# A gated linear attention followed by a switch mixture of experts: experts ranked by count, rows turned on VectorE, products and moves rearranged

## The chip, the cores and the metric

The kernel runs on one core of one Trainium2 chip. The metric is device time in microseconds, the median of several runs; a profiled execution gives the span and everything inside it. All data are float32 in device memory.

## The reference

```python
# attention, (4, 8, 768, 48) each: q, k, v, a_re, a_im
mag = sqrt(a_re**2 + a_im**2); scale = minimum(mag, 0.999) / (mag + 1e-6)
for t in range(S):
    new_re = ar * S_re - ai * S_im
    new_im = ar * S_im + ai * S_re
    S_re, S_im = new_re + k[t] (outer) v[t], new_im
    y[t] = q[t] @ S_re
# x = y as (3072 tokens, 384)
logits = x @ w_gate                     # 8 experts
expert_idx = argmax(logits); gate_w = softmax(logits) at expert_idx
for e in range(8):
    h = maximum(x[mask] @ w1[e], 0)     # 384 x 1024
    out[mask] = gate_w[mask] * (h @ w2[e])   # 1024 x 384
```

## The kernel before

**Stage 1, attention** (0 to 239.8 us of the span). The complex decay is turned into magnitudes and angles along time, so that q and k are multiplied by decay and rotation, and a chunked linear attention follows. `front(u)` prepares one of ten units of time (`UNITS`, 128 to 384 steps of a batch; n = 3 x T columns, 1152 for a full unit). It loads gates (AB) and q, k (Z), takes logarithms and exponentials on ScalarE, and on VectorE runs two scans (L284 of the decay, L295 of the angle), the range reduction (L300, L301), the clipping L282, and the products by `mul` and `tt` (all at L150): im x c (here product 1), k x a, q x c (product 6), then z times cosine into `hz` and z times sine in place. Products 1 and 6 go to GpSimd (POOL) from unit `EARLY` = 3 on. The heads lie packed on 128 partitions (`BLOCKS`: p0, p1, g0, g1, h0, d0), and DMAs issued by SP (L334) move them to `hz`, with a real and an imaginary part for each head on 96 partitions: nine for a unit. `chunk(b, c)` does the attention of 128 steps on TensorE (L361 to L403), and `route` (L423 to L464) the gate, the expert and the place of each token; GpSimd scatters the rows into `xs_hbm`, where each expert has `CAP` = 448 places (L464). Places that may stay free are filled beforehand by DMAs from `empty`. The order of all this on every engine is a list written out by hand (`ORDER`, base 36 numbers of the operations), so an engine takes its work as listed, and waits where an input is late. After the last chunk some small VectorE operations and two products (L513 to L535) decide whether the slow, exact path `again` has to follow.

**Stage 2, experts** (239.8 us to the end). `expert(e)` loads w1 (L572), w2 (L574), 384 rows (L575) and the last 64 (L578) by SP. TensorE transposes the rows (L586), VectorE and ScalarE copy them out (L588). For each of eight hidden blocks three products with 448 columns (L597) follow and a rectification (L600, L603); three output blocks of 128 tokens take eight products of 384 columns each (L611). The 64 tokens behind 384 of two experts share one output bank (L626), one expert on each half of its partitions. VectorE applies the gate (L566), and GpSimd scatters into the output (L555). Here `Plan.order()` lists the operations, greedily by earliest start and then by longest tail, from the durations given to `M.add`. Three buffers hold w1 and three w2; xr, xrt and ht have two each. Two PSUM banks take transposes, three hidden blocks and three outputs. A product of L597, L611 or L626 in float32 leaves two records in the trace.

## Time and profile before

| | |
|---|---|
| median of 3 runs | 570.27 us (564.31 to 571.41) |
| profiled execution | 565.04 us, span 563.2 us |
| mean granted clock of TensorE | 0.967 |
| busy over the span | PE 86%, DVE 43%, ACT 38%, POOL 17% |
| attention | 0 to 239.8 us |
| experts | 239.8 us to the end |
| moved by DMA | 82.03 MB, mean 146 GB/s |

PE is TensorE, PEld its loading of weights, DVE VectorE, ACT ScalarE, POOL GpSimd and SP the engine that issues most DMAs (SPq in a timeline is its queue of commands). [...] The 16 DMA engines have a share of 1.00 when all are busy. The shares over the span are averages of two stages with different limits, so rows are read by stage. The duration of a matmul's record is modelled and overlaps its neighbours; starts are better compared with starts.

### The profile page before, as it was taken

Reading aid. Unit: us, or ns where it says so; the run is one execution under the profiler, and the core shown is the slowest. Engines: PE = TensorE matmul, PEld = TensorE weight load, DVE = VectorE, ACT = ScalarE, POOL = GpSimd, SP = SyncE. Lnnn points to the kernel's source line nnn. Section 1 sums busy time; section 2 is a strip of 40 time slices with the busy share of each in tenths; the row PEclk is TensorE's granted clock in tenths of the full one; section 3 lists DMA queues with packets and bytes.
Section 4 is the critical chain, followed back from the end, with each engine's and each line's share of the span. In section 5 each row is a group of like instructions: output and inputs, shape, how many; then the busy total and the mean of one; then the engine's idle time right before and its main releaser. Section 6 shows DMA issues by size and latency. Waiting matters only on the chain. (4 is left out here: it accounts for less than half of the span.)

```text
span 563.2 us, 7082 instructions
## 1 busy us (share of the span) xinstructions
PE 485.5 (86%) x2785; PEld 329.1 (58%) x2785; DVE 240.8 (43%) x412; ACT 214.0 (38%) x313; POOL 94.3 (17%) x106
## 2 busy tenths in 40 slices
PE   0045998798898799729999999999999999999995
PEld 0034997787798699614555555555555555555552
DVE  3999989989798684401111021110111011211011
ACT  6999898979788565201100011000011000111000
POOL 3012214206240533200001020020100010200022
PEclk9999999989799799959999999999999999999998
DMA  8486959578399865199502272214443021400010
GB/s 320 131 252 163 256 149 336 116 214 216 118 208 217 245 113 180 44 318 387 205 14 82 111 263 64 98 42 169 160 143 120 14 69 57 145 2 14 1 38 34
DMA packets 25384, 82.03 MB, mean 146 GB/s; under 512 B 3600, under 2 KB 16816, under 8 KB 20896
## 3 DMA queue, kind: packets, MB, share of 16 engines
q1 hardware_dynamic: 22016, 72.04, 42.8%
q0 software_dynamic: 3328, 9.47, 4.6%
q8 instruction: 24, 0.39, 0.3%
q14 instruction: 16, 0.13, 0.1%
HBM read 54.32 MB, written 12.62 MB: 119 GB/s over the span
## 5 line engine op out<-in xcount | busy, mean ns | idle before, releaser
L597 PE MATMUL bank<-xrt,w1b 128*128 128x448 f32 x384 | 149.4, 544 | 2.1 <-ACT xrt L588 2.1
L611 PE MATMUL bank<-w2b,ht 128*128 128x384 f32 x384 | 128.4, 488 | 0.0
L597 PEld LDWEIGHTS bank<-xrt,w1b 128*128 128x128 f32 x384 | 73.0, 192 | 70.5 <-issue 64.8
L611 PEld LDWEIGHTS bank<-w2b,ht 128*128 128x128 f32 x384 | 72.1, 190 | 51.9 <-issue 6.9
L603 ACT ACTIVATE ht<-bank 128x448 f32<-128x448 f32 x32 | 17.4, 544 | 174.0 <-PE bank L597 174.0
L555 POOL DMA_INDIRECT out_dram<-yo,xr x24 | 23.5, 978 | 292.2 <-DVE yo L566 288.1
L368 PE MATMUL bank<-hz 96*128 96x128 f32 x384 | 61.6, 315 | 7.7 <-DMA hz<-Z 6.5
L600 DVE TENSOR_SCALAR ht<-bank 128x448 f32<-128x448 f32 x32 | 20.0, 625 | 111.4 <-PE bank L597 111.4
L368 PEld LDWEIGHTS bank<-hz 96*128 96x128 f32 x384 | 54.8, 221 | 12.0 <-issue 6.1
L361 PE MATMUL bank<-ident,hz 96*128 96x96 f32 x160 | 23.6, 279 | 38.0 <-DMA hz<-Z 35.4
L566 DVE TENSOR_SCALAR yo<-bank,xr 128x384 f32<-128x384 f32 x24 | 14.8, 618 | 79.4 <-PE bank L611 79.4
L588 ACT COPY xrt<-bank 128x384 f32<-128x384 f32 x16 | 7.6, 478 | 94.0 <-PE bank L586 93.9
L361 PEld LDWEIGHTS bank<-ident,hz 96*128 96x128 f32 x160 | 18.7, 161 | 40.6 <-issue 38.1
L236 ACT ACTIVATE AB<-AB 128x1152 f32<-128x1152 f32 (+2 forms) x40 | 38.3, 968 | 7.1 <-DMA AB<-in_gates_u_dram 5.2
L150 DVE TENSOR_TENSOR am<-bank,causal 128x512 f32<-128x512 f32 x48 | 32.3, 680 | 14.5 <-PE bank L368 14.5
L150 DVE TENSOR_TENSOR Z<-Z,AB 128x1152 f32<-128x1152 f32 (+4 forms) x20 | 34.1, 1704 | 1.2 <-DMA hz<-Z 0.3
L403 PE MATMUL bank<-turn,yt 128*128 128x104 f32 x192 | 28.0, 292 | 6.7 <-ACT yt L391 3.9
L464 POOL DMA_INDIRECT xs_hbm<-xg,slot x24 | 26.1, 1088 | 40.1 <-DVE cumb L461 14.8
L150 POOL TENSOR_TENSOR AB<-AB,C 128x1152 f32<-128x1152 f32 (+2 forms) x7 | 18.0, 2567 | 87.3 <-ACT C L236 77.2
L387 PE MATMUL bank<-am,v 128*48 128x128 f32 x384 | 30.5, 299 | 2.2 <-DVE am L150 2.2
L395 PE MATMUL bank<-v,kt 128*96 128x48 f32 x320 | 31.6, 253 | 0.0
L395 PEld LDWEIGHTS bank<-v,kt 128*96 128x96 f32 x320 | 30.1, 171 | 1.8 <-issue 1.5
(110 smaller groups left out, 499.3 us busy)
## 6 DMA issues: line engine op xcount, KB each, us to landing
w1b<-in_w_dram SPq DMA_DIRECT2D x8, 1536.0 KB, 14.0
w2b<-in_w_dram SPq DMA_DIRECT2D x8, 1536.0 KB, 7.0
AB<-in_gates_u_dram SPq DMA_DIRECT2D x6, 1152.0 KB, 7.1
Z<-in_qk_u_dram SPq DMA_DIRECT2D x6, 1152.0 KB, 8.2
hz<-Z SPq DMA_DIRECT2D x12, 432.0 KB, 8.7
xr<-xs_hbm SPq DMA_DIRECT2D x8, 579.0 KB, 7.8
v<-in_v_dram SPq DMA_DIRECT2D x8, 576.0 KB
hz<-hz SPq DMA_DIRECT2D x6, 432.0 KB, 5.5
```

Of the source, the lines that this page charges most:

```text
L150: (eng or nc.vector).tensor_tensor(out=o, in0=a, in1=b, op=op)
L236: lambda: nc.scalar.activation(o, i, func=f, scale=scale, bias=bias, **kw), r, w, tag)
L361: nc.tensor.transpose(KT[hf][:, (h % 4) * 96:(h % 4) * 96 + 96], hk[:, h], ident[0:96, 0:96])
L368: nc.tensor.matmul(SC[hf][:, (h % 4) * 128:(h % 4) * 128 + 128], lhsT=hk[:, h], rhs=hq[:, h], start=True, stop=True)
L387: nc.tensor.matmul(YT[ps, (h // 2) * 128:(h // 2) * 128 + 128], lhsT=V[:, cl, h * D:h * D + D], rhs=am[2 * par + hf][:, h % 4, :], start=( ...
L395: nc.tensor.matmul(ST[0:96, h * D:h * D + D], lhsT=kt[par][:, h * 96:h * 96 + 96], rhs=V[:, cl, h * D:h * D + D], start=(c == 0 and h == 0 ...
L403: nc.tensor.matmul(XT[:, p * 104:p * 104 + 104], lhsT=yt[par][:, p * 128:p * 128 + 128], rhs=turn[:, p, :], start=True, stop=True)
L464: i = nc.gpsimd.indirect_dma_start(out=xs_hbm[:, :], out_offset=bass.IndirectOffsetOnAxis(ap=R[slot][:, c:c + 1], axis=0), in_=xg[:, (g0 + ...
L555: i = nc.gpsimd.indirect_dma_start(out=out[:, :], out_offset=bass.IndirectOffsetOnAxis(ap=index, axis=0), in_=y, in_offset=None, bounds_ch ...
L597: nc.tensor.matmul(HB[hb][:, 0:CAP], lhsT=w1b[ws][:, c:c + 128], rhs=xrt[s][:, d, :], start=(d == 0), stop=(d == DT - 1))
L600: M.add("DVE", 0.6, lambda f_=f_, hb=hb: nc.vector.tensor_scalar_max(ht[s][:, f_, :], HB[hb][:, 0:CAP], 0.0), (("H", hb),), (("ht", s, f_),))
L611: nc.tensor.matmul(OB[ob][:, 0:DM], lhsT=ht[s][:, f_, j * 128:j * 128 + 128], rhs=w2b[ws][:, f_ * DM:f_ * DM + DM], start=(f_ == 0), stop= ...
```

## The change

**In attention.** Heads 6 and 7 are packed so that their last 16 channels alternate on partitions 96 to 127, and the moves of a unit become seven (three real, four imaginary). Product 1 is always on VectorE; product 6 is on GpSimd from unit 1 on. Each GpSimd product waits, by an added dependence, for the last VectorE operation with `port=True` that the list has ahead of it. The fills become two of 80 places for each expert, from place `MINC` = 288 on. The first expert's weights (`wA1`, `wA2`, expert 0) are loaded in unit 4. The list `ORDER` is a new one (its numbers are not shown).

**Ranking.** After the last route, VectorE ranks the experts by count, expert 0 kept first, and `perm` holds the expert of each rank. SP reads it into a register (`values_load`) and addresses rows and weights by it. Rank r has `ROOM[r]` places (448, 448, 416 four times, 384, 384), and `again` also follows if a count exceeds its room.

**Experts.** The rows are loaded by four DMAs an expert, each to 32 partitions, with 288 numbers of a row in one piece; VectorE turns 32x32 blocks (`nc.vector.transpose`, three an expert) into what the products read. Gates and places come by DMAs of their own (`hg`, `hs`). The tokens behind 384 go to `hl`, and share two output banks: 64 each of ranks 0 and 1, 32 each of ranks 2 to 5. Hidden and output blocks have four PSUM banks each; w1b has two buffers and w2b five.

```diff
+BLOCKS = [x for g in range(3) for x in ((slice(0, 48), g, g, 0), (slice(48, 96), g, 3 + g, 0))]
+BLOCKS += [(slice(96, 128), 0, 6, 0), (slice(96, 128), 1, 7, 0), (slice(96, 128, 2), 2, 6, 32), (slice(97, 128, 2), 2, 7, 32)]
-EARLY = 3
+EARLY = 1
+ON_POOL = "6"
-MINC = 256
+MINC = 288
+FIRST = 0
+ROOM = (448, 448, 416, 416, 416, 416, 384, 384)
+LEFT = ((0, 0, 64, 0, 0), (1, 0, 64, 0, 64), (2, 0, 32, 1, 0), (3, 0, 32, 1, 32), (4, 0, 32, 1, 64), (5, 0, 32, 1, 96))
+XW = 288
...
-            mul(pool, n, im, im, c, (Bk, Ck), (Bk,))
+            mul(pool1, n, im, im, c, (Bk, Ck), (Bk,))
...
-            mul(pool, n, qq, qq, c, (Q, Ck), (Q,))
+            mul(pool6, n, qq, qq, c, (Q, Ck), (Q,))
...
+                pieces = ([(0, 48, 0)] if part else []) + [(48, 96, 3)]
+                todo = [(hz[slot][r0:r0 + D, h0:h0 + 3, :, off:off + T], src[p0:p1], range(h0, h0 + 3), 0) for p0, p1, h0 in pieces]
+                todo.append((hz[slot][r0:r0 + 32, 6:8, :, off:off + T], src[96:128, 0:2], (6, 7), 0))
+                todo.append((hz[slot][r0 + 32:r0 + 48, 6:8, :, off:off + T], src[96:128, 2], (6, 7), 32))
...
+                if u == 4:
+                    for o, src, k in ((wA1, w1, "wA1"), (wA2, w2, "wA2")):
+                        P.add("SP", 0.65, lambda o=o, src=src: nc.sync.dma_start(o, src[FIRST * 128:FIRST * 128 + 128, :]), (), (k,),
...
-                o["fn"]()
+                ins = o["fn"]()
+                if o["port"] and o["eng"] == "DVE":
+                    behind = ins
+                elif o["port"] and behind is not None:
+                    tc.add_manual_dep(ins.ins, behind.ins.name, mybir.DependencyInfo(mybir.DependencyClass.Sync, mybir.DependencyReason.DATA),
...
+            for q in range(4):
+                M.add("SP", 0.65, lambda q=q: nc.sync.dma_start(
+                    xr[s][32 * q:32 * q + 32, 0:nb, :], row(r, 0, 32 * nb).rearrange("(b p) w -> p b w", p=32)[:, :, 32 * q:32 * q + XW]),
...
+            for d in range(DT):
+                M.add("DVE", 0.00105 * nt + 0.06, lambda d=d: nc.vector.transpose(
+                    xrt[s][:, d, 0:nt].rearrange("p (b i) -> p b i", i=32), xr[s][:, 0:nb, d * 128:d * 128 + 32]),
...
-                        nc.tensor.matmul(HB[hb][:, 0:CAP], lhsT=w1b[ws][:, c:c + 128], rhs=xrt[s][:, d, :], start=(d == 0), stop=(d == DT - 1))
+                        nc.tensor.matmul(HB[hb][:, 0:nt], lhsT=a[:, c:c + 128], rhs=xrt[s][:, d, 0:nt], start=(d == 0), stop=(d == DT - 1))
...
+                    for rr, n, p0 in who:
+                        nc.tensor.matmul(OB[ob][p0:p0 + n, 0:DM], lhsT=hl[sh][:, f_, p0:p0 + n], rhs=w2_of(rr)[0][:, f_ * DM:f_ * DM + DM],
+                                         start=(f_ == 0), stop=(f_ == FT - 1), skip_group_check=True)
```

TensorE where the first expert passes into the second (L586 transposes, L597 hidden products, L611 outputs), before:

```order
L597 MATMUL bank_63<-xrt_1983,w1b_1975 128x448 x3
L586 MATMUL bank_61<-ident,xr_1982 128x128 x3
L586 MATMUL bank_62<-ident,xr_1982 128x128 x3
L597 MATMUL bank_64<-xrt_1983,w1b_1975 128x448 x3
L586 MATMUL bank_61<-ident,xr_1982 128x128 x3
L586 MATMUL bank_62<-ident,xr_1982 128x64 x3
L611 MATMUL bank_66<-w2b_1978,ht_1985 128x384 x4
L597 MATMUL bank_65<-xrt_1984,w1b_1976 128x448 x3
```

The same place after the change (L663 hidden products, L679 outputs; wA the early weights of the first expert):

```order
L663 MATMUL bank_61<-xrt_1996,wA_127 128x448 x3
L663 MATMUL bank_63<-xrt_1996,wA_127 128x448 x3
L663 MATMUL bank_62<-xrt_1997,w1b_1988 128x448 x3
L663 MATMUL bank_64<-xrt_1997,w1b_1988 128x448 x3
L663 MATMUL bank_61<-xrt_1997,w1b_1988 128x448 x3
L663 MATMUL bank_63<-xrt_1997,w1b_1988 128x448 x3
L663 MATMUL bank_61<-xrt_1997,w1b_1988 128x448 x3
L663 MATMUL bank_62<-xrt_1997,w1b_1988 128x448 x3
L663 MATMUL bank_63<-xrt_1997,w1b_1988 128x448 x3
L663 MATMUL bank_64<-xrt_1997,w1b_1988 128x448 x3
L679 MATMUL bank_65<-wA_128,ht_1998 128x384 x4
L679 MATMUL bank_66<-wA_128,ht_1998 128x384 x4
```

The transposes are gone, the first expert's products read weights that came in attention, and all hidden blocks of the second expert now stand ahead of the first expert's outputs.

The second shared group on TensorE after the change (L692; hl holds the hidden values of the tokens behind 384), the first six of 32 commands:

```order
L692 MATMUL bank_68<-w2b_1991,hl_2001 32x384
L692 MATMUL bank_68<-w2b_1992,hl_2001 32x384
L692 MATMUL bank_68<-w2b_1993,hl_2001 32x384
L692 MATMUL bank_68<-w2b_1989,hl_2001 32x384
L692 MATMUL bank_68<-w2b_1991,hl_2001 32x384
L692 MATMUL bank_68<-w2b_1992,hl_2001 32x384
```

Four experts' products of 32 columns stand one after another, where pairs of 64 stood in L626.

SP's commands at the start of the expert stage, before (L572 w1, L574 w2, L575 and L578 rows):

```order
L572 DMA w1b_1975<-in_w_dram 128x3072
L575 DMA xr_1981<-xs_hbm 128x3x386
L578 DMA xr_1981<-xs_hbm 64x386
L574 DMA w2b_1978<-in_w_dram 128x3072
L575 DMA xr_1982<-xs_hbm 128x3x386
L578 DMA xr_1982<-xs_hbm 64x386
```

After (L632 rows, L627 the register with the rank's expert, L636 w1; ISA computes an address):

```order
L632 DMA xr_1994<-xs_hbm 32x14x288 x4
L627 TENSOR_LOAD perm
L636 ISA
L636 DMA w1b_1988<-in_w_dram 128x3072
L632 ISA
L632 DMA xr_1995<-xs_hbm 32x14x288
```

Nothing stands ahead of the first rows now; the second expert's commands stand behind the register, and its w1 ahead of its rows.

GpSimd's products in attention, the first five before (AB by C is product 1, Z by C product 6):

```order
L150 TENSOR_TENSOR AB_125<-AB_125,C_131 128x1152
L150 TENSOR_TENSOR AB_126<-AB_126,C_132 128x1152
L150 TENSOR_TENSOR Z_128<-Z_128,C_131 128x3x384
L150 TENSOR_TENSOR AB_127<-AB_127,C_133 128x1152
L150 TENSOR_TENSOR Z_129<-Z_129,C_132 128x3x384
```

and after:

```order
L156 TENSOR_TENSOR Z_144<-Z_144,C_147 128x3x256
L156 TENSOR_TENSOR Z_145<-Z_145,C_148 128x3x384
L156 TENSOR_TENSOR Z_143<-Z_143,C_146 128x3x384
L156 TENSOR_TENSOR Z_144<-Z_144,C_147 128x3x384
L156 TENSOR_TENSOR Z_145<-Z_145,C_148 128x3x384
```

VectorE after the change, in the same part of attention:

```order
L294 SCALAR_TENSOR_TENSOR AB_140<-C_146,AB_140 128x1152
L156 TENSOR_TENSOR Z_145<-Z_145,AB_142 128x3x384
L315 TENSOR_SCALAR AB_142<-AB_142 128x1152
L156 TENSOR_TENSOR am_154<-bank_62,causal 128x512
L297 TENSOR_SCALAR AB_140<-AB_140 128x1152
L316 SCALAR_TENSOR_TENSOR AB_142<-AB_142 128x1152
L299 SCALAR_TENSOR_TENSOR AB_140<-AB_140,lend,C_146 128x384
L156 TENSOR_TENSOR AB_141<-AB_141,C_147 128x1152
```

Product 1 (the last row, AB_141 by C) has come to VectorE, where Z_145 by AB_142 is k x a, and GpSimd's row has product 6 alone.

## Rows read from the trace of the kernel before

**Rows 1.** Stage windows: us, busy per engine (records), granted PE clock, DMA share, GB/s.
```profile
28.00:141.00 113.00, 91.90 (x855) 82.67 (x855) 107.20 (x125) 102.61 (x129) 29.00 (x14) 0.98 0.77 213
...
239.80:252.90 13.10, 2.89 (x12) 2.07 (x13) 1.21 (x4) 0.96 (x2) 0.00 (x0) 0.50 0.96 325
252.90:557.20 304.30, 302.65 (x980) 163.20 (x980) 44.26 (x81) 23.79 (x46) 25.45 (x26) 1.00 0.29 103
...
168.96:183.04 14.08, 12.58 (x153) 11.91 (x153) 12.08 (x21) 11.94 (x20) 1.11 (x1) 1.00 1.00 217
...
255.90:270.20 14.30, 14.30 (x39) 7.17 (x38) 2.04 (x4) 1.63 (x3) 0.00 (x0) 1.00 1.00 401
```

**Rows 2.** Groups by line, expert stage: busy us, mean ns, idle before and releaser.
```profile
L597 PE MATMUL bank<-xrt,w1b 128*128 128x448 f32 x384 | 149.4, 544 | 2.1 <-ACT xrt L588 2.1
...
L626 PE MATMUL bank<-w2b,ht 128*64 128x384 f32 x128 | 21.5, 489 | 0.0
...
L586 PE MATMUL bank<-ident,xr 128*128 128x128 f32 (+1 forms) x96 | 14.4, 282 | 9.8 <-DMA xr<-xs_hbm 9.8
```

**Rows 3.** TensorE's timeline: start us, duration us, line, records, [idle <-releaser].
```profile
252.90 17.51 PE L597 MATMUL bank<-xrt,w1b 128*128 128x448 f32 x42 [0.50 <-ACT xrt L588]
...
330.57 16.05 PE L597 MATMUL bank<-xrt,w1b 128*128 128x448 f32 x42 [0.57 <-ACT xrt L588]
...
365.05 6.93 PE L597 MATMUL bank<-xrt,w1b 128*128 128x448 f32 x18
371.82 5.32 PE L611 MATMUL bank<-w2b,ht 128*128 128x384 f32 x16
...
406.71 16.02 PE L597 MATMUL bank<-xrt,w1b 128*128 128x448 f32 x42 [0.50 <-ACT xrt L588]
```

**Rows 4.** All engines, timeline where attention ends and the expert stage begins.
```profile
241.67 0.38 SPq L575 DMA_DIRECT2D xr<-xs_hbm  x1
...
249.52 2.89 PE L586 MATMUL bank<-ident,xr 128*128 128x128 f32 x12 [9.77 <-DMA xr<-xs_hbm]
```

**Rows 5.** The same view at the end of the span.
```profile
558.05 0.98 POOL L555 DMA_INDIRECT out_dram<-yo,xr  x1 [1.60 <-DVEq L645]
559.33 0.98 POOL L555 DMA_INDIRECT out_dram<-yo,hg  x1 [0.30 <-issue]
```

**Rows 6.** The same view in attention: products on GpSimd beside VectorE.
```profile
61.60 2.67 POOL L150 TENSOR_TENSOR Z<-Z,C 128x1152 f32<-128x1152 f32 x1 [11.43 <-ACT C L236]
61.69 1.92 DVE L295 TENSOR_TENSOR_SCAN AB<-bank,tend,AB 128x384 f32<-128x384 f32 x2
...
91.88 3.33 POOL L150 TENSOR_TENSOR AB<-AB,C 128x1152 f32<-128x1152 f32 x1 [3.73 <-DVE AB L300]
...
92.70 3.72 DVE L301 SCALAR_TENSOR_TENSOR AB<-AB 128x1152 f32<-128x1152 f32 x1
...
117.99 1.36 DVE L301 SCALAR_TENSOR_TENSOR AB<-AB 128x1152 f32<-128x1152 f32 x1
119.27 0.75 DVE L282 TENSOR_SCALAR AB<-AB 128x1152 f32<-128x1152 f32 x1
```

**Rows 7.** VectorE's groups by line and shape, 28 to 213.7 us.
```profile
L150 DVE TENSOR_TENSOR Z<-Z,AB 128x2304 f32<-128x2304 f32 x6 | 17.6, 2933 | 0.5
...
L150 DVE TENSOR_TENSOR hz<-Z,AB 128x2304 f32<-128x2304 f32 x6 | 15.3, 2550 | 1.7 <-ACT AB L236 1.6
L301 DVE SCALAR_TENSOR_TENSOR AB<-AB 128x1152 f32<-128x1152 f32 x6 | 10.5, 1753 | 0.1
...
L282 DVE TENSOR_SCALAR AB<-AB 128x1152 f32<-128x1152 f32 x6 | 6.7, 1113 | 0.0
...
L150 DVE TENSOR_TENSOR Z<-Z,C 128x1152 f32<-128x1152 f32 x1 | 1.4, 1351 | 0.0
```

**Rows 8.** The moves' line L334: count, issue ns (min/median/max), and landing.
```profile
L334 SPq DMA_DIRECT2D hz<-Z x50: 507/592/2177, 25.7 to 220.0; - x50
...
DMA to landing us min/median/max: 2.3/5.0/10.0
```

More of the change, by code (lines that the diff above doesn't have):

```diff
@@ L189, in gateloop_then_moe @@
     ones_b = const([128, 128], "ones_b", 1.0, BF16)
+    num_i = const([128, E], "num_i", dt=I32)
+    nc.gpsimd.iota(num_i, pattern=[[1, E]], base=0, channel_multiplier=0)
+    num = const([128, E], "num")
+    nc.vector.tensor_copy(num, num_i)
+    room = const([128, E], "room")
+    for r in range(E):
+        nc.gpsimd.memset(room[:, r:r + 1], float(ROOM[r]))
+    wA1, wA2 = const([128, DT * F], "wA1"), const([128, FT * DM], "wA2")
     cum = const([128, E], "cum")
@@ L329, in front @@
                     rd = (Q, K) if part else ht_
[L330 removed]
+                    if part and hs[0] == 0:
                         rd = rd + tuple(("hm", slot, cl + x) for x in range(nch))
[L332 removed]
+                    if not part and hs[0] == 3:
                         w = w + tuple(("hm", slot, cl + x) for x in range(nch))
[L334 to L335 removed]
@@ L336, in front @@
-                    moved.setdefault(u, []).append(i)
+                    P.add("SP", 0.65, lambda o=o, i_=i_: nc.sync.dma_start(o, i_), rd, w, lat=1.8,
+                          kb=2 * (48 if d0 == 0 and hs[0] < 6 else 32 if d0 == 0 else 16) * len(hs) * T * 4 / 1e3, rate=(200.0, 250.0, 280.0)[nch - 1])
         def load_v(b, half):
@@ L499, in gateloop_then_moe @@
                             route(b, r0, r1)
+            behind = None
             for i in P.order(ORDER):
@@ new lines, in expert @@
+        def expert(r):
+            nt = ROOM[r]
+            nb = nt // 32
+            s = r % 2
+            (a, ka), (w, kw) = w1_of(r), w2_of(r)
+            for d in range(DT):
+                M.add("DVE", 0.00105 * nt + 0.06, lambda d=d: nc.vector.transpose(
+                    xrt[s][:, d, 0:nt].rearrange("p (b i) -> p b i", i=32), xr[s][:, 0:nb, d * 128:d * 128 + 32]),
+                    tuple(("xr", s, q) for q in range(4)), (("xrt", s, d),))
+            mine = [(k, n, sh, p0) for rr, k, n, sh, p0 in LEFT if rr == r]
@@ L637, in gateloop_then_moe @@
+        with tc.manual_schedule():
+            M.add("SP", 0.0, lambda: None, (), ("perm",))
+            loads(0)
+            for r in range(E):
+                if r + 1 < E:
+                    loads(r + 1)
+                expert(r)
+                for sh in range(2):
+                    if max(x[0] for x in LEFT if x[3] == sh) == r:
+                        shared(sh)
+                if r < E - 1:
                     M.add("POOL", 1.0, lambda: nc.gpsimd.drain(), ("scattered",), ("drained",))
-                if e == 2:
+                if r == 2:
@@ L756, in _layout @@
         z = _np.zeros((B, 128, G, S), a.dtype)
-        for p0, p1, g0, g1, h0, d0 in BLOCKS:
-            z[:, p0:p1, g0:g1] = a[:, h0:h0 + g1 - g0, :, d0:d0 + p1 - p0].transpose(0, 3, 1, 2)
+        for sl, g, h, d0 in BLOCKS:
+            n = len(range(128)[sl])
+            z[:, sl, g] = a[:, h, :, d0:d0 + n].transpose(0, 2, 1)
         a = z
```

295 lines of the change are left out of this document (154 added, 141 removed).

## The prediction

> **What bounds the kernel now.** I read the stage windows first, then the groups of the expert stage by line, then TensorE's own timeline there, and last the hand-over between the stages, the end, and the collisions of VectorE and GpSimd. The windows split the span in three. From 28 to 141 us VectorE is busy 107.2 of 113.0 us and ScalarE 102.6: attention is bound by those two. From 239.8 to 252.9 us TensorE works 2.9 of 13.1 us: it waits for the first expert's rows. From 252.9 to 557.2 us it is busy 302.65 of 304.3 us with DMA share 0.29: a pure TensorE bound [rows 1]. So a product taken out of that last stretch shortens the kernel by its whole length, and the same holds for VectorE's work up to 141 us. What goes beside these costs nothing.
>
> The reader should take cadences and not mean durations, since matmuls overlap: 18 records of L597 from 365.05 to 371.82 us are 6.77 us, 0.376 us for each record of 448 columns, against a mean of 544 ns by line [rows 2, 3].
>
> **Narrower rooms.** There are 384 records of L597 [rows 2]: 384 x 0.376 = 144.4 us. Columns fall from 3584 to 3328 (the sum of ROOM), so 144.4 x 256/3584 = **-10.3 us**. The products of L611 stay (3 x 128 tokens an expert). The rooms hold if the counts fit; the inputs give 354 tokens to the first expert and 421, 406, 403, 392, 388, 370, 338 to the rest in order, so the slow path is not entered.
>
> **Transposes off TensorE.** L586 is busy 14.4 us [rows 2], of which 2.89 us lie ahead of the first product [rows 4]; 11.5 us lie in the bound stretch. The first product behind a copied block also waits for ScalarE, 0.50 us at 406.71 us [rows 3], 2.1 us in all of which 0.5 at the start [rows 2]. So 13.1 us would go if no records overlapped; they do, at both ends of each of some fifteen groups. Between 11.5 and 13.1 I take **-11.8 us**, near the busy time. The work that replaces them, three transposes of up to 448 elements an expert on VectorE, is in no trace here: an estimate of 0.3 to 0.6 us each. From 252.9 us on VectorE is busy 44.3 of 304.3 us [rows 1] and the rows land an expert ahead, so they are hidden; without this cover one expert's three would cost at most 2 us, 14 us over seven.
>
> **Leftover tokens.** Four shared groups cost 21.5 us for 128 records, 5.4 us for the 32 of each [rows 2]. In such a group the two 64-wide products of a pair run side by side: 32 records one after the other at a 384-column cadence of near 0.32 us (0.376 x 384/448) would take 10.3 us. Now there are two groups: one of two experts with 64 tokens (5.4 us as before) and one of four experts with 32 tokens, 64 records. No row has a 32-wide stationary. If four run at once it takes 5.4 us, if still two at a time 10.7 us. I take 6.1 us, near the lower end, because the pair's row shows products of different columns wholly beside each other. 21.5 - 11.5 = **-10.0 us**.
>
> [...]
>
> **Clock.** [...] **+1 us**, bounds 0 and +1.5.
>
> **The start of the expert stage.** The first expert's weights are now loaded in attention (3.1 MB), so rows alone are waited for, but these grow: four transfers of 32 partitions write 2.06 MB in pieces of 1152 B where one of 0.58 MB stood. Before, the rows are asked for at 241.67 us and TensorE begins at 249.52, with weights in front of them; the first product follows 3.38 us later [rows 3, 4]. Now: 241.67 + 2.3 (shortest landing of a move [rows 8]) + 2.06 MB at a rate + three transposes and hand-overs (1.9 us, an estimate: three of 0.5 and 0.4 for the hand-overs). At 401 GB/s, the rate beside a full DMA share later, this is 251.0; at 217 GB/s, the lowest rate at share 1.00 [rows 1], it is 255.4. Bounds -1.9 and +2.5; I take **+1 us**, since small pieces lie nearer the low-rate row. The ranking adds some nine VectorE operations ahead of the registers, but only rank 1 and later wait for them, and they lie beside the first rows' flight.
>
> [...] No trace here shows a 32-partition load alone.
>
> Late next would be the second expert, whose hidden blocks stand right behind the first's on TensorE: its w1 and rows are 3.6 MB, 13.4 us at 401 and 217 GB/s (1.57 and 2.06 MB), and the first expert's 48 hidden records cover 18 us (48 x 0.376). So even at the low rate nothing waits.
>
> **The end.** Behind the last output product there are two scatters, 558.05 and 559.33 us [rows 5], because the shared group ends just ahead. Its groups now come after ranks 1 and 5, so one scatter is left: **-1.3 us**.
>
> **Attention.** Product 1 (im x c) goes from GpSimd to VectorE in seven units; their widths make six times 128x1152, at 1.351 us a row of that shape [rows 7]: +8.1 us. Product 6 (q x c) leaves VectorE in units 1 and 2, 768 and 1152 wide: -2.3 us. VectorE thus has +5.8 us where it is 95% busy. Against it stand collisions: at 91.88 us GpSimd's product and VectorE's L301 overlap, and L301 lasts 3.72 us, where it takes 1.36 us alone at 117.99; at 61.60 us a product runs beside scans, which are not slowed [rows 6]. In sums: L301 1152 wide 10.5 us for six where 8.2 would do, the 2304-wide products in place (Z) 17.6 us where those into hz take 15.3, L282 6.7 us where six of 0.75 would be 4.5 [rows 6, 7]: 6.8 us. Of fourteen GpSimd products nine remain, each made to wait for a listed VectorE operation so that it starts beside scans or reads of PSUM. If that works, about 5 us come back. Behind a waiting GpSimd product stand its scatters of routed rows, which are waited for only at the end of attention. The moves are merged, 90 to 70, at 0.59 us of SP each [rows 8]; two at each hand-over that TensorE or the next load waits for make about 1 us. So **0 us** in all, with bounds of -6 (no collision left, and three hand-overs more that gain from shorter queues of moves, an estimate) and +7 (collisions as often as before, and 1 us for GpSimd's waits). The early weights (7.8 us of a full queue at 401 GB/s) have the slack of 141 to 239.8 us; the narrower fills save 0.4 MB.
>
> **Sum.** -10.3 - 11.8 - 10.0 + 1 + 1 - 1.3 + 0 = -31.4 us against the profiled execution's own 565.04 us: 533.6, so **534 us**. The three runs shown have a median of 570.27; against that the same change would read about 539, inside the range.
>
> **Rivals.** (B) Attention pays. Product 1 on VectorE costs its 5.8 us net and the collisions stay at 6.8 us: 539. If six of the nine products left hold a VectorE operation as at 92.70 (2.36 us each, 14.2 in all), it is 5.8 + 14.2 - 6.8 = 13.2 us: 547. For it speaks that VectorE has only 5.8 us idle from 28 to 141 us [rows 1]; against it, that the 61.60 row shows a product that harms no scan [rows 6]. (C) The narrow group runs two at a time: 10.7 us for 6.1, 538. For it: no row has 32 columns; against it: the pair's row. (D) The loads become the bound of the expert stage. An expert brings 5.06 MB (3.15 of weights, up to 2.06 of rows less what a narrow room saves). TensorE's stage of about 272 us gives each 34 us, so loads decide below 149 GB/s. At 133 GB/s the stage is 31.4 us longer and the gain gone (565); below 129 GB/s the kernel is more than 2% slower, at 127 it is at 580. Against it: 217 GB/s is the lowest rate at a full share, 401 the highest [rows 1]; for it: pieces of 1152 B out of rows 1544 B apart were never loaded so.
>
> **Chances.** Forecast 0.75, B 0.13, C 0.04, D 0.08 (0.05 at about no change, 0.03 slower). The forecast's own range is 523 (533.6 - 0.7 - 1 - 2.9 - 6, the lower bounds of the narrow group, clock, start and attention) to 543 (+ 0.5 + 1.5 + 7 at the upper ones). With B to its upper part the range is 523 to 548; it leaves out D and about a tenth of the rest. A measurement of this kernel tells about 2% from no change; faster by over 2% ends at 553.7, and all but D lie under it: faster 0.92, same 0.05, slower 0.03.
>
> **What would show it.** In the changed profile: TensorE 99% busy from its first hidden product to the end in about 273 us; no transposes among its rows; hidden records at 0.35 us for 416 columns; the group with four experts near 6 us (C: 10.7, every second pair of records beside each other); first product between 251 and 255.4 us; one scatter behind the last output. VectorE's 28 to 141 us stretch should end at the same time with no L316-type row (the former L301) beyond 2 us (B: several of 3 us, and the expert stage starts 6 us or more later). Under D TensorE's rows would show waits for rows or weights at every expert's start, and DMA share 1.00 there. The forecast is wrong if the stage's shortening is not the sum of the three cuts on TensorE.

## The result and the profile after

The changed kernel takes 534.38 us (median of 4 runs, 528.76 to 541.95) where the kernel before takes 567.29 (median of 4, 560.00 to 571.41): a ratio of 0.943 with a 95% interval of 0.924 to 0.962, taken over the two faster executions of each kernel. Its profiled execution took 528.76 us, with a span of 527.0 us against 563.2. Attention's length differs by up to 26 us between profiles of kernels with the same attention code (see "Attention's spread" below), so below stages are compared with stages and not whole times.

The stage windows after (columns as in [rows 1]):

```profile
0.00:234.00 234.00, 177.49 (x1791) 161.50 (x1791) 192.74 (x321) 188.24 (x265) 53.78 (x81) 0.96 0.73 209
```

```profile
28.00:141.00 113.00, 91.17 (x891) 82.43 (x891) 109.45 (x129) 106.03 (x133) 24.13 (x13) 0.98 0.86 235
...
234.00:250.78 16.78, 0.19 (x2) 0.09 (x2) 3.96 (x25) 0.00 (x0) 0.99 (x1) 0.50 0.84 193
250.78:521.73 270.95, 270.94 (x864) 150.88 (x864) 48.31 (x104) 18.45 (x56) 24.43 (x25) 0.99 0.53 144
521.73:527.00 5.27, 0.01 (x1) 0.00 (x0) 0.62 (x1) 0.00 (x0) 0.98 (x1) 0.72 0.18 60
```

The reader sees that TensorE is busy 270.94 of 270.95 us from its first hidden product to its last output, with a DMA share of 0.53 (before 302.65 of 304.3 at 0.29 [rows 1]). VectorE is busy 109.45 of 113 us up to 141 us, as full as before.

TensorE's timeline after (columns as in [rows 3]); L663 are hidden products, L692 leftovers:

```profile
250.78 20.07 PE L663 MATMUL bank<-xrt,wA 128*128 128x448 f32 x48 [13.11 <-DVE xrt L652]
270.69 18.20 PE L663 MATMUL bank<-xrt,w1b 128*128 128x448 f32 x48
...
371.62 8.54 PE L663 MATMUL bank<-xrt,w1b 128*128 128x416 f32 x24
380.00 10.48 PE L679 MATMUL bank<-w2b,ht 128*128 128x384 f32 x32
...
433.61 5.37 PE L692 MATMUL bank<-w2b,hl 128*32 128x384 f32 x64
438.91 15.75 PE L679 MATMUL bank<-w2b,ht 128*128 128x384 f32 x48
...
506.09 15.64 PE L679 MATMUL bank<-w2b,ht 128*128 128x384 f32 x48
```

The first 48 records take 20.07 us and the next 48 take 18.20. A narrow room's 24 records (416 columns) take 8.38 us start to start, 371.62 to 380.00, 0.349 us each. The group of four experts takes 5.30 us, 433.61 to 438.91. No row is a transpose.

Where attention passes into the experts, and at the end (the same view, all engines; they answer to [rows 4, 5]):

```profile
234.26 0.99 POOL L475 DMA_INDIRECT xs_hbm<-xg,slot  x1 [3.99 <-DVE f L563]
...
237.01 2.12 SPq L632 DMA_DIRECT2D xr<-xs_hbm  x4
...
250.09 1.70 DVE L652 STREAM_TRANSPOSE xrt<-xr 128x448 f32<-128x448 f32 x3 [12.23 <-DMA xr<-xs_hbm]
```

```profile
522.67 0.98 POOL L596 DMA_INDIRECT out_dram<-yo,hg  x1 [1.60 <-POOLq L717]
```

The last rows are scattered at 234.26 us (238.48 before), the four row loads are issued from 237.01 us, and VectorE turns them at 250.09: 13 us for 2.06 MB. In windows of 2 us between 239 and 249 us the DMA engines move 190 to 241 GB/s at a full share, as here:

```profile
239.00:241.00 2.00, 0.00 (x0) 0.00 (x0) 0.00 (x0) 0.00 (x0) 0.00 (x0) 0.50 1.10 241
241.00:243.00 2.00, 0.00 (x0) 0.00 (x0) 0.00 (x0) 0.00 (x0) 0.00 (x0) 0.50 1.08 190
```

One scatter is left behind the last output.

By stages the span falls by 36.2 us: 4.2 up to the last scatter of rows, -2.1 (a loss) from there to the first hidden product, 33.3 from the first hidden product to the end of the last output (304.22, 252.90 to 557.12, against 270.95), and 0.8 behind it (6.1 against 5.3).

### The profile page after: what moved, and what is told of

Read it like the earlier page. It is cut to its first block, busy times and chain, and to the rows that moved or that the text cites. A ratio compares the mean times of both kernels' runs of the same rounds, so it can differ in the third digit from the quotient of the medians.

```text
span 527.0 us, 6989 instructions
## 1 busy us (share of the span) xinstructions
PE 448.6 (85%) x2657; PEld 312.5 (59%) x2657; DVE 245.6 (47%) x449; ACT 206.7 (39%) x321; POOL 80.2 (15%) x108
## 5 line engine op out<-in xcount | busy, mean ns | idle before, releaser
L663 PE MATMUL bank<-xrt,w1b 128*128 128x416 f32 (+2 forms) x336 | 118.3, 509 | 0.0
L679 PE MATMUL bank<-w2b,ht 128*128 128x384 f32 x336 | 110.8, 487 | 0.0
L671 ACT ACTIVATE ht<-bank 128x384 f32<-128x384 f32 x32 | 15.7, 490 | 232.4 <-PE bank L663 219.9
L663 PEld LDWEIGHTS bank<-xrt,w1b 128*128 128x128 f32 x336 | 63.9, 190 | 52.0 <-issue 37.5
L679 PEld LDWEIGHTS bank<-w2b,ht 128*128 128x128 f32 x336 | 63.9, 190 | 45.1 <-issue 2.9
L596 POOL DMA_INDIRECT out_dram<-yo,hg x24 | 23.5, 977 | 262.4 <-DVE yo L607 172.2
L668 DVE TENSOR_SCALAR ht<-bank 128x384 f32<-128x384 f32 x32 | 17.6, 556 | 88.2 <-PE bank L663 88.2
L607 DVE TENSOR_SCALAR yo<-bank,hg 128x384 f32<-128x384 f32 x24 | 14.8, 618 | 89.5 <-PE bank L679 89.5
L156 POOL TENSOR_TENSOR Z<-Z,C 128x1152 f32<-128x1152 f32 (+2 forms) x9 | 20.5, 2277 | 132.1 <-ACT C L250 40.5
L475 POOL DMA_INDIRECT xs_hbm<-xg,slot x24 | 27.4, 1142 | 47.3 <-DVE lg L420 17.7
L663 PE MATMUL bank<-xrt,wA 128*128 128x448 f32 x48 | 20.1, 582 | 13.1 <-DVE xrt L652 13.1
L414 PEld LDWEIGHTS bank<-turn,yt 128*128 128x128 f32 x192 | 25.2, 204 | 5.1 <-ACT yt L402 3.5
L652 DVE STREAM_TRANSPOSE xrt<-xr 128x416 f32<-128x416 f32 (+2 forms) x24 | 13.2, 590 | 30.5 <-DMA xr<-xs_hbm 25.3
## 6 DMA issues: line engine op xcount, KB each, us to landing
Z<-in_qk_u_dram SPq DMA_DIRECT2D x6, 1152.0 KB, 11.8
```

The costliest lines, as they stand in the source:

```text
L156: return (eng or nc.vector).tensor_tensor(out=o, in0=a, in1=b, op=op)
L414: nc.tensor.matmul(XT[:, p * 104:p * 104 + 104], lhsT=yt[par][:, p * 128:p * 128 + 128], rhs=turn[:, p, :], start=True, stop=True)
L475: i = nc.gpsimd.indirect_dma_start(out=xs_hbm[:, :], out_offset=bass.IndirectOffsetOnAxis(ap=R[slot][:, c:c + 1], axis=0), in_=xg[:, (g0 + ...
L596: i = nc.gpsimd.indirect_dma_start(out=out[:, :], out_offset=bass.IndirectOffsetOnAxis(ap=index, axis=0), in_=y, in_offset=None, bounds_ch ...
L663: nc.tensor.matmul(HB[hb][:, 0:nt], lhsT=a[:, c:c + 128], rhs=xrt[s][:, d, 0:nt], start=(d == 0), stop=(d == DT - 1))
L668: M.add("DVE", 0.00105 * n + 0.12, lambda o=o, k=k, n=n, hb=hb: nc.vector.tensor_scalar_max(o, HB[hb][:, k:k + n], 0.0), (("H", hb),), (ko,))
```

## The experiments

All are the changed kernel with one edit, unless said, and each gave one profile. The kernel before, run beside them, took 567 to 577 us, so their own times are not compared with 534; only e12 and e13 were run often enough (six times each) for a ratio. Two marks serve: the last scatter of rows on GpSimd (L475) and the first hidden product on TensorE.

**The rooms (e4).**

```diff
-ROOM = (448, 448, 416, 416, 416, 416, 384, 384)
+ROOM = (448,) * 8
```

> The changed kernel with 448 places for every rank (ROOM), so that all hidden products have 448 columns and all loads and transposes 448 rows. Theory A (TensorE is the only bound of the expert stage): its length from the first hidden product to the last output grows from 270.95 us by 256 columns at 0.376 us for 448 and 48 records an expert, 10.3 us, to 281.2, with TensorE without waits. Theory B (loads had become a second bound): more than 12 us, with waits for rows at the start of an expert.

TensorE's timeline of e4, its first and its last row:

```profile
271.95 20.65 PE L663 MATMUL bank<-xrt,wA 128*128 128x448 f32 x48 [13.03 <-DVE xrt L652]
...
535.50 18.22 PE L679 MATMUL bank<-w2b,ht 128*128 128x384 f32 x56
```

The stage lasts from 271.95 to 553.72, 281.77 us: 10.8 more than 270.95. Of these, 0.6 us lie in the first 48 records, which have 448 columns in both kernels (20.65 us here, 20.07 there; no run shows what lengthened them). So the narrow rooms are worth 10.2 us, against 10.3 by theory A. TensorE's timeline has no wait between these two rows, and loading and turning 448 rows for all costs no more than the 0.6 us above: the loads are no bound even when they grow.

**The clock at the start (e2).**

```diff
+        for i in range(15):
+            nc.tensor.matmul(bank[7][:, 0:384], lhsT=wA1[:, 0:128], rhs=wA1[:, 0:384], start=True, stop=True)
         M = Plan()
```

> The changed kernel with fifteen products on the early weights (128 x 384, their result is not used) on TensorE between the ranking and the first hidden product. The first 48 hidden records take 20.07 us in the changed kernel, the next 48 take 18.20. Theory A (the loss is the low clock behind an idle TensorE): the first 48 take 18.2 to 18.5 us and the stage is 1.6 to 1.9 us shorter. Theory B (the loss is something else at the start, such as the loads at a full DMA share beside the products): 20 us as before.

```profile
259.12 11.55 PE L594 MATMUL bank<-wA 128*128 128x384 f32 x30 [0.24 <-DVE again L576]
271.94 18.31 PE L665 MATMUL bank<-xrt,wA 128*128 128x448 f32 x48 [1.28 <-DVE xrt L654]
290.08 18.20 PE L665 MATMUL bank<-xrt,w1b 128*128 128x448 f32 x48
```

In the changed kernel the granted clock, a share of full speed, reads 0.50 from 250.78 to 253 us, 0.66 to 255 us and 1.00 to 257 us. In e2, with TensorE busy from 259.12 us on, the first 48 records take 18.31 us instead of 20.07, and the whole stage 269.19 (271.94 to 541.13) instead of 270.95. Theory A by its numbers; e12 below, with five such products, shows the clock with them: it reads 0.98 from 258 to 264 us, and its first 48 records take 18.31 us too.

**The first rows (e1, e5, e10).** What holds the first hidden product back for 16.5 us? In e1 two of the four loads go by ScalarE's queue:

```diff
-                M.add("SP", 0.65, lambda q=q: nc.sync.dma_start(
+                M.add("ACT" if r == 0 and q > 1 else "SP", 0.65, lambda q=q: (nc.scalar if r == 0 and q > 1 else nc.sync).dma_start(
```

> The changed kernel, but of the first expert's four row loads the two for partitions 64 to 127 are issued by ScalarE's queue, so that they run beside the two for partitions 0 to 63. In the changed kernel the rows take from 237.0 to 250.0 us, 2.06 MB at 190 to 230 GB/s with every DMA engine busy. [...] Theory B (the rate is set by the pieces of 1152 B or by reads 1544 B apart): the rate stays near 200 GB/s, 16.5 us within 0.7, or a little more since the next weights now compete.

The last scatter is at 246.56 and the first product at 264.54 us, 17.98 us: later, not sooner. But this doesn't settle the cause. Windows of 2 us of e1:

```profile
253.00:255.00 2.00, 0.00 (x0) 0.00 (x0) 0.00 (x0) 0.00 (x0) 0.00 (x0) 0.50 1.08 213
...
257.00:259.00 2.00, 0.00 (x0) 0.00 (x0) 0.00 (x0) 0.00 (x0) 0.00 (x0) 0.50 1.18 400
```

While the rows were in flight with the second expert's w1, the rate rose from 213 to 400 GB/s: together they went faster than one after the other, but the rows were no longer first, so theory B does not describe what happened. What holds the rows alone to 190 to 241 GB/s in the changed kernel no run shows.

In e5 the first expert's weights are loaded after the ranking, w1 ahead of the rows:

```diff
-                        P.add("SP", 0.65, lambda o=o, src=src: nc.sync.dma_start(o, src[FIRST * 128:FIRST * 128 + 128, :]), (), (k,),
+                        P.add("SP", 0.65, lambda: None, (), (k,),
...
+                for at, o, src in ((0, wA1, w1), (7, wA2, w2)):
+                    if 4 * r + q == at:
+                        i = nc.sync.dma_start(o, src[FIRST * 128:FIRST * 128 + 128, :])
...
```

> The changed kernel with the first expert's weights loaded behind the ranking instead of in attention: its w1 ahead of the first rows, its w2 behind the second expert's third row load. In the changed kernel the first hidden product starts 16.5 us after the last scatter of rows is issued, after 13 us of row loads at about 200 GB/s. Theory A (loads in one queue follow one another): 1.57 MB at 400 GB/s more, the first product 20 to 21 us after the last scatter, and the second expert's rows, 1.57 MB later in the queue too, wait less than 3 us more. [...]

The first product came at 277.83 us, 20.3 us after the last scatter at 257.57, and the second expert waited for nothing: theory A. So loading these weights in attention is worth 3.7 us; without it the larger row loads would have cost 5.8 us against before instead of 2.1.

In e10 the first expert's rows come only as the numbers that are used, half of them by ScalarE's queue:

```diff
...
+                        M.add(e_, 0.65, lambda q=q, d=d, k_=k_: k_.dma_start(
+                            xr[s][32 * q:32 * q + 32, 0:nb, 128 * d:128 * d + 32],
+                            row(r, 0, 32 * nb).rearrange("(b p) w -> p b w", p=32)[:, :, 128 * d + 32 * q:128 * d + 32 * q + 32]),
...
```

> The changed kernel, but the first expert's rows come only as the 96 numbers of a row that each quarter of the partitions needs, in three pieces of 128 B (0.69 MB in 5376 pieces) instead of one of 1152 B (2.06 MB in 1792 pieces), six transfers by SP and six by ScalarE's queue. In the changed kernel the first hidden product starts 16.5 us after the last scatter of rows, behind 10 us of row loads at about 200 GB/s. Theory A (each piece costs a DMA engine a time of its own beside its bytes: 1792 pieces in 10.3 us on 16 engines are 92 ns a piece, where 1152 B at the 400 GB/s of the weights would be 46): 5376 pieces of about 50 ns are 17 us, the first product 22 to 25 us after the last scatter. Theory B (the bytes decide, at 200 GB/s for this pattern): 0.69 MB in 3.5 us and the issue of six transfers, the first product 10 to 13 us after the last scatter.

TensorE and GpSimd in e10 (two timelines), and a window of its row loads:

```profile
260.00 0.98 POOL L475 DMA_INDIRECT xs_hbm<-xg,slot  x1 [4.75 <-DVE f L563]
```

```profile
268.97 19.69 PE L671 MATMUL bank<-xrt,wA 128*128 128x448 f32 x48 [5.56 <-DVE xrt L660]
```

```profile
265.00:267.00 2.00, 0.00 (x0) 0.00 (x0) 0.00 (x0) 0.00 (x0) 0.00 (x0) 0.50 1.25 181
```

The first product starts 8.97 us after the last scatter, 7.5 us sooner than in the changed kernel, and below what theory B allowed. The rate is 168 to 181 GB/s with pieces of 128 B, not much under the 190 to 241 with 1152 B: here bytes decide and not the number of pieces. The second queue alone, in e1, had brought nothing. Two thirds of what the changed kernel loads for each expert are numbers that nothing reads.

**GpSimd's order (e3).**

```diff
-                elif o["port"] and behind is not None:
-                    tc.add_manual_dep(ins.ins, behind.ins.name, mybir.DependencyInfo(mybir.DependencyClass.Sync, mybir.DependencyReason.DATA),
...
```

> The changed kernel without the added dependence of GpSimd's products on VectorE's listed operation. Theory A (the order is what took the collisions away): VectorE's operations of 1152 and 2304 columns grow again by 2 to 3 us where a GpSimd product meets them, 2 to 6 us in all, and the last scatter of rows is issued 1 to 5 us later than at 234.26 us. Theory B (nine products instead of fourteen and the new list alone did it): no such operation grows, the last scatter within 1 us.

VectorE and GpSimd in e3 (timeline), a collision that is in none of the runs with the order (the same VectorE operation takes 0.95 us at 27.93 in the changed kernel, with no product beside it):

```profile
198.54 3.05 DVE L316 SCALAR_TENSOR_TENSOR AB<-AB 128x768 f32<-128x768 f32 x1
198.95 1.82 POOL L156 TENSOR_TENSOR Z<-Z,C 128x768 f32<-128x768 f32 x1
```

Five VectorE operations outlast others of their shape by 0.7 us or more (three in the changed kernel, seven before), and VectorE's busy time up to the last scatter is 196.3 us, against 193.1 in e4, whose attention is that of the changed kernel. So the order takes about 3 us of collisions away. The last scatter, at 255.62 us, is within 0.2 us of e2 (255.46) and e4 (255.50), which have the order. The theories each fail by half: the collisions return, the time doesn't, which fits a pace that TensorE at its low clock sets in all three (e4's windows below); no run took that apart.

**Product 1 (e6).**

```diff
-ON_POOL = "6"
+ON_POOL = "16"
```

> The changed kernel with product 1 back on GpSimd from unit 1 on, ordered as product 6 is. VectorE has 8 us less, GpSimd 18 to 20 us more. Theory A (VectorE's 5.8 us net are paid for by fewer collisions): VectorE's busy time in attention falls by 8.1 us less 3 to 6 us of new collisions, and since this product is twice as long on GpSimd (2.6 us) and ScalarE waits for it, the start of the third unit's work, and the first chunks, come 0 to 4 us later. Theory B (product 1 on VectorE is a loss that other parts of the change hide): the first chunks start 2 us or more sooner than at 42.2 and 60.5 us.

```profile
128.71 2.63 POOL L156 TENSOR_TENSOR AB<-AB,C 128x1152 f32<-128x1152 f32 x1 [5.66 <-ACT AB L250]
...
130.17 3.58 DVE L156 TENSOR_TENSOR hz<-Z,AB 128x2304 f32<-128x2304 f32 x1 [0.32 <-issue]
...
138.97 2.66 POOL L156 TENSOR_TENSOR Z<-Z,C 128x1152 f32<-128x1152 f32 x1
...
139.85 3.00 DVE L294 SCALAR_TENSOR_TENSOR AB<-C,AB 128x1152 f32<-128x1152 f32 x1
```

VectorE's first operations on the chunks' scores start later from the beginning (45.6 and 65.0 us instead of 42.2 and 60.5). VectorE's busy time in attention is 193.1 us, no less than in the changed kernel (192.7): the 8.1 us of products that left it came back as longer operations (theory A had 3 to 6 us coming back), as at 130.17 (3.58 us, alone 2.55 [rows 7]) and 139.85 (3.00, alone 1.35 at 42.79 in the changed kernel). So on this list product 1 costs VectorE the same on either engine, and on GpSimd the chain is longer.

**Attention's spread (e8, e9, e11).** With the same attention code the last scatter stands at 234.26 us in the changed kernel, at 246.56 in e1, 255.46 in e2, 255.50 in e4 and 260.00 in e10 (and at 257.57 in e5, without the two weight loads). Each is a single profile of another kernel; the four executions of the changed kernel itself have spans of 527.0 to 540.2 us. The 6 us windows show where (columns as in [rows 1]); first the changed kernel, then e4:

```profile
108.00:114.00 6.00, 3.91 (x49) 3.29 (x48) 6.00 (x14) 4.75 (x9) 2.85 (x2) 1.00 0.96 265
114.00:120.00 6.00, 6.00 (x50) 5.66 (x49) 5.48 (x8) 4.51 (x6) 3.25 (x2) 0.72 0.68 246
120.00:126.00 6.00, 5.91 (x60) 5.12 (x60) 5.61 (x8) 5.79 (x9) 4.66 (x3) 1.00 0.31 113
```

```profile
108.00:114.00 6.00, 3.91 (x48) 3.29 (x47) 6.00 (x14) 4.76 (x8) 2.84 (x2) 0.91 1.05 301
114.00:120.00 6.00, 6.00 (x36) 5.76 (x38) 4.83 (x9) 3.92 (x7) 3.31 (x3) 0.50 0.63 249
120.00:126.00 6.00, 6.00 (x37) 5.05 (x33) 2.90 (x3) 5.25 (x6) 3.29 (x2) 0.50 0.26 99
126.00:132.00 6.00, 6.00 (x35) 5.41 (x35) 4.91 (x5) 1.22 (x4) 0.00 (x0) 0.50 0.01 3
132.00:138.00 6.00, 6.00 (x40) 5.90 (x40) 4.37 (x4) 4.83 (x5) 1.35 (x1) 0.50 0.76 140
```

In both TensorE is idle for 2.1 of the 6 us from 108 us. Then the granted clock falls, to 0.72 for one window here and to 0.50 for four there, in which TensorE is busy 6.00 of 6 us and VectorE 2.90 to 4.91. Why it recovers so much sooner here, behind the same wait, no run shows; and a wait as long can be followed by no fall at all (the changed kernel again):

```profile
186.00:192.00 6.00, 4.02 (x36) 3.69 (x37) 4.55 (x10) 1.92 (x5) 3.39 (x4) 1.00 0.95 339
192.00:198.00 6.00, 6.00 (x65) 5.43 (x64) 4.08 (x8) 5.97 (x10) 1.80 (x1) 1.00 0.08 28
```

How long the clock was low goes with the spread. Added up over such windows from 36 us to the last scatter (each window's length times twice what the clock lacks to 1.00, an estimate), the time at 0.50 is 17 us in the changed kernel, 37 in e1, 57 in e4 and 63 in e10: the order of their last scatters, and 46 us more of it stand beside 25.7 us more of attention. e2, with 38 us, also had slow records early on (last section).

What TensorE waits for at 111.5 us is a chain that begins on VectorE (all engines, the changed kernel):

```profile
108.65 2.71 POOL L156 TENSOR_TENSOR Z<-Z,C 128x1152 f32<-128x1152 f32 x1 [23.99 <-DVE m L434]
...
108.78 2.61 DVE L442 TENSOR_SCALAR sm<-sm 128x6 f32<-128x6 f32 x1
...
113.67 1.13 PEld L414 LDWEIGHTS bank<-turn,yt 128*128 128x128 f32 x8 [2.22 <-ACT yt L402]
```

GpSimd's product starts at 108.65 us, and an operation of six columns that starts 0.13 us later lasts 2.61 us (0.16 us at 166.30, with no product beside it); behind it come the chunk's reduction, ScalarE's copies and TensorE's weight load at 113.67 (the last row), after 2.22 us of waiting. The order put GpSimd behind a large operation, but small ones are not in it. e8 leaves this small operation out:

```diff
-            dv(0.2, lambda: nc.vector.tensor_scalar_add(R["sm"], R["sm"], 1e-9), ("sm",), ("sm",))
+            dv(0.2, lambda: None, ("sm",), ("sm",))
```

> The changed kernel without the one small VectorE operation of each route that adds 1e-9 to the sum of exponentials (the sum is at least 1, so a float32 does not see it). In the changed kernel and in three experiments with the same attention it starts 0.13 us behind GpSimd's product at about 108.7 us and lasts 2.61 us instead of 0.16; TensorE then waits 2.09 us for ScalarE's copy before the product of chunk 7, and in the next 6 us the granted clock is 0.50 to 0.75. Theory A (this wait is what the clock falls behind): the wait is under 0.7 us, the clock from 114 to 120 us (or 7 us later, where TensorE rose late) is 1.00, and the last scatter of rows is issued 3 us or more before the same point of the other runs (234.26 and 246.56 where TensorE rose early, 255.5 where it rose late). Theory B (the clock falls on its own account): the wait is gone and 2 us are saved, but the clock falls within some us of the same place.

```profile
114.00:120.00 6.00, 6.00 (x72) 5.41 (x71) 5.97 (x15) 5.97 (x12) 0.64 (x1) 1.00 1.02 324
120.00:126.00 6.00, 5.27 (x46) 4.94 (x46) 5.27 (x10) 5.91 (x8) 2.21 (x2) 0.76 0.99 322
```

Here TensorE's early records stayed slow up to 90 us (35 to 42 in each 6 us from 60 us, 53 to 71 in the changed kernel), so the place is reached some 9 us later, in the second window. TensorE waits 0.73 us in it instead of 2.09, and the clock falls all the same, to 0.76 and 0.95 in the windows from 120 and 126 us; the last scatter is at 255.51 us, as in e2 and e4, so the 2 us that theory B saved do not show either. That is nearer to theory B. e9 keeps the small operation, and keeps TensorE busy instead:

```diff
             def f():
+                for p in range(10 if gc == 7 else 0):
+                    nc.tensor.matmul(XT[:, 416:512], lhsT=ident, rhs=ident[:, 0:96], start=True, stop=True)
```

> The changed kernel with ten products on the identity (their result is not used), about 2 us, ahead of chunk 7's L414, in the time in which TensorE waits 2.09 us for ScalarE. Nothing else is moved. Theory A (idleness of TensorE is what the clock falls behind): the granted clock stays at 1.00 from 114 to 120 us (0.50 to 0.75 in the runs without), and chunk 8 starts 1 to 8 us sooner behind chunk 7. Theory B (the clock falls whether TensorE works or not): 0.50 to 0.75 as before.

```profile
108.00:114.00 6.00, 5.54 (x63) 4.92 (x62) 6.00 (x14) 4.75 (x9) 2.84 (x2) 1.00 0.97 288
114.00:120.00 6.00, 6.00 (x67) 5.59 (x68) 5.93 (x9) 5.53 (x8) 3.77 (x3) 1.00 0.60 243
120.00:126.00 6.00, 5.91 (x61) 5.23 (x57) 6.00 (x7) 5.80 (x9) 3.65 (x3) 1.00 0.28 102
```

The clock stays at 1.00 there, in all windows up to 156 us, and so at 140 to 155 us too, where the changed kernel fell again. Then it falls at other waits, to 0.75 at 162 and to 0.50 from 210 us, and the last scatter is at 242.82 us: sooner than in e4, but later than in the changed kernel, which had the fall. e11 fills six such places, the first ahead of chunk 0, and has the edits of e2 and e8; one of its fills:

```diff
+                    for p in range({0: 7, 1: 10}.get(gc, 0) if hf == 0 else 0):
+                        nc.tensor.matmul(XT[:, 416:512], lhsT=ident, rhs=ident[:, 0:96], start=True, stop=True)
```

> The changed kernel without the small operation of e8, with the products of e2 ahead of the first hidden product, and with products whose results are not used in five places of attention where TensorE waited in the runs before: 42 ahead of the first chunk (to 39 us), 7 and 10 in chunks 0 and 1, 5 ahead of chunk 12's transposes, 4 and 15 ahead of L414 in chunks 7 and 21. Theory A (the low clock follows an idle TensorE, and attention's length from 234 to 257 us with the same code is the sum of these falls): records are short from the first chunk on (under 120 ns each from 60 us), the stretch 114 to 126 us stays at 1.00, and the last scatter is issued at 225 to 236 us. Theory B (the falls come from something else, such as what the chip grants for a work done): falls to 0.50 stay, at the same or other places, and the last scatter is issued after 242 us.

The window from 114 to 126 us stays at 1.00, but the clock falls to 0.62 in the window from 48 us and 0.50 in the next, behind waits in chunk 0 (TensorE busy 2.60 of 6 us from 42 us, 4.08 in the changed kernel), and to 0.50 at 210 us behind waits that were not filled. The last scatter is at 246.72 us: theory B by its number. So in e9 a filled wait kept the clock up at its place, where it fell in the four kernels that reached it at the same time without a fill (the changed kernel, e1, e4, e10), and the fall came at a later wait; filling some of them is not worth much. That the fills did the same in e11 is not shown: e12 below, without one in attention, is at 1.00 from 84 to 144 us.

**Together (e12, e13).** e12 has the edit of e10, that of e8, and five of e2's products:

```diff
+        for i in range(5):
+            nc.tensor.matmul(bank[7][:, 0:384], lhsT=wA1[:, 0:128], rhs=wA1[:, 0:384], start=True, stop=True)
```

e13 has e11's fills as well, with more of them in chunk 0 (against e11), none in chunk 1, and ten in chunk 20 for the 15 in chunk 21:

```diff
-                    for p in range({0: 7, 1: 10}.get(gc, 0) if hf == 0 else 0):
+                    for p in range({(0, 0): 7, (0, 1): 15}.get((gc, hf), 0)):
```

> The changed kernel with three edits of the experiments together: the first expert's rows in pieces of 128 B (7.5 us in e10), five products on the early weights ahead of the first hidden product (1.8 us in e2 with fifteen; the stretch is now 5 us), and without the small operation (2 us of wait in chunk 7). Nothing in attention keeps TensorE busy. The sum is 9 to 11 us beside the changed kernel, whose ratio to the kernel before was 0.943: 0.92 to 0.93. The first hidden product starts 8.5 to 9.5 us after the last scatter of rows, and the expert stage lasts 269 to 270 us. If the small pieces only moved the wait (to the second expert), the stage is longer than 272 us.

```profile
254.80 5.19 PE L594 MATMUL bank<-wA 128*128 128x384 f32 x10 [0.24 <-DVE again L576]
260.29 18.31 PE L673 MATMUL bank<-xrt,wA 128*128 128x448 f32 x48 [0.29 <-DVE xrt L662]
278.43 18.20 PE L673 MATMUL bank<-xrt,w1b 128*128 128x448 f32 x48
```

Its last scatter is at 251.15 us, the first hidden product 9.14 us later, its first 48 records take 18.31 us, and its stage 269.19 us (260.29 to 529.48). Its ratio to the kernel before is 0.923 (0.918 to 0.929; 532.56 us, where before took 577.15 in the same runs). That is about 2% below the 0.943 of the changed kernel, but the two intervals overlap (0.924 to 0.929), so the times do not show a gain; the stages put it at 9.1 us, 7.4 at the start and 1.8 in the expert stage.

> As e12, with products whose results are not used where TensorE waited in attention: 42 ahead of the first chunk, 7 and 15 in chunk 0, 4 and 10 ahead of L414 in chunks 7 and 20, 5 ahead of chunk 12's transposes. Theory A (falls of the clock follow such waits and make most of attention's spread): ratio 0.89 to 0.915, 1 to 3% below e12, with records short from the first chunks on and no fall at 114 or 210 us. Theory B (the falls come anyway, or the added products cost what they save): within 1% of e12, or above it.

The ratio is 0.930 (0.924 to 0.935; 534.51 us): not below e12, as theory B has it. The last scatter is at 245.98 us. Its profile shows full speed from 84 to 162 us, the place at 114 us among it (e12's from 84 to 144), but the clock is at 0.53 in the window from 48 us, at 0.50 in those from 66 and 72 us, behind waits between the early products and the first regular chunks.

## Why the prediction was right

The change is faster by more than 2%, and 534 us was forecast where the median is 534.38. By its own sum, made against the profiled 565.04 us, it gave 533.6 where the profiled execution after took 528.76: 4.9 us more was gained than summed. That the median lies within 0.4 us of 534 is luck: the executions go from 528.76 to 541.95, and 4.2 of the 4.9 us lie in attention, where they are not shown to be the change's. The three cuts on TensorE, less the clock, were summed to 31.1 us and gave 33.3. Point by point:

| term | predicted, us | measured, us |
|---|---|---|
| narrower rooms | -10.3 | -10.2 (e4) |
| transposes off TensorE | -11.8 | -12.8 (the rest of 33.3) |
| leftovers, two groups | -10.0 | -10.6 (21.2 to 10.6) |
| low clock, more than before | +1 | +0.4 (1.87 against 1.46) |
| start, from the last scatter | +1 | +2.1 (16.52 against 14.42) |
| end | -1.3 | -0.8 (6.1 to 5.3) |
| attention | 0 | -4.2 in this execution |

- The bound was read right: TensorE has no wait in 270.95 us, so all that left it came off the time. The transposes' line is what is left of 33.3 when the measured others are taken (33.27 - 10.24 - 10.63 + 0.41 = 12.81); no run measured it alone. By starts, the fourteen groups of L586 behind 252.9 us held TensorE for 11.6 us with their waits, and the 384 output records, the same work before and after, take 0.95 us less without them (125.23 to 124.28). So the upper part of the stated 11.5 to 13.1 was nearer than 11.8.
- A group of the kernel before takes 5.31 us by starts, four of them 21.2:

```profile
317.94 5.38 PE L626 MATMUL bank<-w2b,ht 128*64 128x384 f32 x32
323.25 2.85 PE L611 MATMUL bank<-w2b,ht 128*128 128x384 f32 x8
```

- Four products of 32 columns do run at once: 64 records in 5.30 us. I took 6.1 and held 10.7 possible; the lower bound was right: four experts take 5.30 us here, and two took 5.31 before. Rival C is out.
- The three transposes on VectorE take 0.58 us each (0.57 to 0.65), within 0.3 to 0.6 but for the longest, and after the first expert nothing waits for them.
- No run shows the +1 us that the sum has for the clock. Before, the first 42 records took 1.46 us more than a later 42 [rows 3], at a granted clock of 0.50 from 239.8 to 255.9 us and 1.00 behind; after, the first 48 take 1.87 us more than the next 48, at 0.50 from 234 to 253 us. So 0.4 us came in its place, and e2 recovers 1.8 us of such a loss.
- The start went to the end of its range: from the first row command to the first product 13.77 us pass (237.01 to 250.78) instead of 11.23 (241.67 to 252.90), the +2.5 of the upper bound; 0.4 of it came back because the command follows the last scatter sooner (2.75 us behind it, before 3.19). At 190 to 241 GB/s the rows came near the low bound's 217, so +1 was a choice too near the middle. What sets that rate is not shown: in e1 the rows shared the flight with the second expert's w1 (213 to 400 GB/s), and e10's smaller pieces came at 168 to 181 GB/s through two queues. The early weights were worth 3.7 us (e5), which the sum did not name as a term.
- Attention: VectorE's busy time up to the last scatter is 192.7 us against 193.7 before. That is the 0 I forecast: +5.8 for the products, and collisions down from about 10 to 5 us (what operations take beyond others of their shape); 2 us more went, which no run takes apart. That the order takes collisions away was right (without it, in e3, VectorE is busy about 3 us longer), but its share on the path cannot be read off: the same code ends between 234.3 and 260.0 us. So the 4.2 us gained in the profiled execution are not shown to be the change's, and my range of -6 to +7 for attention was far too narrow for one execution. The step that failed is that I took VectorE and ScalarE for the only bounds there: at a granted clock of 0.50 TensorE is busy 6.00 of 6 us, VectorE 2.90 to 4.91 (e4's windows from 114 us), so I take TensorE to set the pace there. The kernel before has such falls, too (TensorE busy 6.00 us, granted 0.50 in the window from 144 to 150 us), which I had not used.
- Rival B did not come, and e6 shows its premise wrong: product 1 on VectorE costs nothing net. Of the former L301 (L316 now) no operation exceeds 1.36 us, as forecast for the case that the order works. Rival D is out: no wait for loads at a DMA share of 0.53, nor with 448 rows for all (e4).
- The end gave 0.8 of 1.3 us: one scatter is gone, as forecast, but behind the last one 4.33 us pass (522.67 to 527.0) instead of 3.87 (559.33 to 563.2).

## What to carry to other kernels

Where one engine is busy without a gap, cadences (start to start) of its record groups gave the gain of what left it to within about a microsecond a term, and the work moved to an idle engine was free here (three transposes of 0.58 us an expert, which TensorE does not wait for after the first). Before loading larger pieces to have fewer of them, measure both: here a third of the bytes in pieces nine times smaller arrived 7.5 us sooner. Where an engine's clock can fall, compare stages of profiles, and not times of single runs, before crediting a change.
